# Seven of nine key chunks, and the pooled queries, turned from rounded copies, with other target times in the order: pooled attention and two MLPs on one core

## Chip, core and metric

One NeuronCore of a Trainium2 chip runs the whole program. The metric is the device time of one execution in microseconds (us). Three runs of the kernel before took 680.78, 680.83 and 681.04 us; the median is 680.83 us.

## What is computed

```python
batch, n_heads, seq, head_dim = (2, 8, 1152, 64)
# _attn_ref
q_pool = q.reshape(B, H, S // factor, factor, D).mean(axis=3)      # factor 2: 576 queries a head
scores = scale * np.matmul(q_pool, k.transpose(0, 1, 3, 2))
scores = scores - np.max(scores, axis=-1, keepdims=True)
attn = np.exp(scores)
attn = attn / (np.sum(attn, axis=-1, keepdims=True) + 1e-09)
out = np.matmul(attn, v)
# the heads are joined to x (1152 x 512), then two MLPs, 512 -> 2048 -> 512
h = x @ w_in;  g = 0 / ((h + 1)**2 / 4) / h by h <= -1, between, >= 1;  x = g @ w_out
h = x @ w_in;  g = h * sigmoid(h);  out = g @ w_out
```

## The kernel before

Every product is made in float32r from operands split into a rounded high part and a rest (`lo_of`, L138).

**Attention, 16 heads.** For a head, `inputs` (L409) loads q, k and v. K is rounded (L446) and its rest taken (L138), the nine chunks of 128 keys are turned by TensorE (L464) and evicted to `kk` (L469) by ScalarE or VectorE. Of the 576 pooled queries 512 are handled here: GpSimd adds the pairs (L481), a DMA doubles the sum beside itself in `qs` (L488), TensorE turns the four tiles of 128 queries in float32 (L496), and ScalarE and VectorE make `qm` of it (L499, L503). The remaining 64 queries of two heads form a tail tile (`pt`, `qts`, L526 to L537).

`scores` (L540) makes, per tile of 128 queries, three products of 384 keys (L570); VectorE evicts each to a tile `p` of 128 x 1152 and keeps the least value (L577, L587); ScalarE takes the exponent in place (L590). There are eight buffers `p`, four to a head. `values` (L618) then takes the nine key chunks c = 0 to 8: TensorE turns the four `p` tiles of a chunk into one bank, the bank is split into high part and rest (`split`, L600: ScalarE and VectorE, or ScalarE and GpSimd), and two products with V follow (L647).

A chunk is turned in one of two ways. Chunks 0 to 3 are turned straight from `p` in float32 (`turn`, L630). Chunks 4 to 8 are turned from a float32r copy (`turn_copy`, L634): after the exponent, SyncE sends two DMAs per tile (L597) that copy chunks 4, 5 to `pr0` and 6, 7, 8 to `pr1`. There is one buffer of each, so a head's copies wait until the head before has been turned from them:

```python
COPIED = ((4, 2), (6, 3))
prs = [pp.tile([P, NM, n * P], F32R, name=f"pr{i}") for i, (_, n) in enumerate(COPIED)]
copy = lambda i=i, c=c, n=n: nc.sync.dma_start(out=prs[i][:, t].bitcast(F32), in_=ps_[pb.slot][:, c * P : (c + n) * P])
```

**MLPs.** There are 96 steps of `gemm1` (L158) and `gemm2` (L203 in the first MLP, L205 in the second). The first four `gemm1` steps are laid between the last heads.

**What sets the order.** All of this is written as a list of operations (`op`, L276 on), each with a target time, the ways in which it can run (engine, occupancy, latency), what it depends on and the buffers it takes. `plan_out` (L262) is a list scheduler: on each engine it takes, among what can start at once, the operation with the least target, and each engine then runs its instructions in that fixed order. SyncE's row of DMA issues is one of these orders too: an issue that waits holds all behind it.

Of the kernel before, what the change touches and what calls it, by code (L numbers as in the profile page):

```python
# [1 line left out]

# [16 lines left out]
def fused_kernel(  # L19
# [11 lines left out]
    nc = tc.nc  # L31
# [22 lines left out]
    WARM = 7  # L54
    COPIED = ((4, 2), (6, 3))
    AHEAD = 3.0
# [208 lines left out]
    def plan_out():  # L265
# [78 lines left out]
    with ExitStack() as at, ExitStack() as keys, ExitStack() as prep:  # L344
# [15 lines left out]
        khls = several(nat, 2, [P, KC, 2, D], F32R, "khl")  # L360
        qss = several(nat, 2, [P, NM, 2, D], F32, "qs")
        kks = several(qk, 3, [P, KC, P], F32R, "kk")
        qms = [several(qk, 2, [P, NM * P], F32R, f"qm{i}") for i in range(2)]
        qts = [several(qk, 2, [P, 3, QT], F32R, f"qt{i}") for i in range(2)]
        ps_ = several(pp, 2 * NM, [P, S], F32, "p")
        pts = several(pp, 1, [P, S], F32, "pt")
# [8 lines left out]
        tiny = fixed.tile([P, 1], F32, name="tiny")  # L375
        room.update(qraw=2, kraw=2, vraw=1, khl=2, qs=2, kk=3, qm=2, qt=2, qtraw=2, qts=1, p=2 * NM, pt=1, **{f"pr{i}": 1 for i in range(len(COPIED))}, thl=THL, pf=PF, vhl=2)
        room.update(y2=2, rb=2, z=1, b=6, y=2, w=1)
# [28 lines left out]
        def base(h):  # L406
            return h * PERIOD

        def inputs(h):  # L409
# [5 lines left out]
            def load(which, dst, src):  # L415
                return lambda: nc.sync.dma_start(out=dst(), in_=src)

            kraw[h] = kr = Buf("kraw")
            queue = ("SP", 1.2, 3.9, nc.sync) if h else ("ACT", 0.1, 3.8, nc.scalar)
            lk = op(t0, (*queue[:3], lambda: queue[3].dma_start(out=kraws[kr.slot], in_=k[b, hd].rearrange("(p c) d -> p c d", c=KC))), bufs=[kr])  # L420
            qraw[h] = qr = Buf("qraw")
            lq = op(
                t0 - 0.1,
                ("SP", 1.1, 3.8, lambda: nc.sync.dma_start(out=qraws[qr.slot], in_=q[b, hd, 0 : 2 * NM * P].rearrange("(t p r) d -> p t r d", p=P, r=2))),
                bufs=[qr],
# [12 lines left out]
            tv = base(h - 2) + (6 if h < 3 else 0)  # L438
            lv = op(tv, ("SP", 1.2, 3.9, lambda: nc.sync.dma_start(out=vraws[vr.slot], in_=v[b, hd].rearrange("(p c) d -> p c d", c=KC))), bufs=[vr])

# [3 lines left out]
            for part in [slice(3 * g, 3 * g + 3) for g in range(3)] if h == 0 else [slice(0, KC)] * 1:  # L444
                n = (part.stop - part.start) / KC
                hi = lambda part=part: nc.scalar.copy(khls[kb.slot][:, part, 0], kraws[kr.slot][:, part])  # L446
                khi.append(op(t1, ("ACT", 0.08 + 0.5 * n, 0.17 + 0.51 * n, hi), [lk], [kr, kb]))
                lo = lambda e, part=part: lambda: lo_of(e, khls[kb.slot][:, part, 1], kraws[kr.slot][:, part], khls[kb.slot][:, part, 0])
                ways = [("POOL", 0.2 + 1.175 * n, 0.25 + 1.18 * n, lo(nc.gpsimd))]
                if not h:  # L450
                    ways.insert(0, ("DVE", 0.1 + 0.6 * n, 0.18 + 0.6 * n, lo(nc.vector)))
                klo.append(op(t1 + 0.01, ways, [khi[-1]], [kr, kb], both=not h))
# [21 lines left out]

            qb, bank, mb = Buf("qs"), Buf("b"), Buf("qm")
            qm[h] = mb

            def split_q(e):
                t = qraws[qr.slot]
                if h:  # L480
                    e.tensor_add(qss[qb.slot][:, :, 0], t[:, :, 0], t[:, :, 1])  # L481
                else:
                    e.tensor_add(qss[qb.slot], *(t[:, :, r].unsqueeze(2).to_broadcast([P, NM, 2, D]) for r in range(2)))

            t3 = base(h - 2) - 0.1 * PERIOD
            if h:
                sq = op(t3, ("POOL", 0.7, 0.76, lambda: split_q(nc.gpsimd)), [lq], [qr, qb])
                twice = lambda: nc.sync.dma_start(out=qss[qb.slot][:, :, 1], in_=qss[qb.slot][:, :, 0])  # L488
                sq = op(t3 + 1, ("SP", 0.5, 2.6, twice), [sq], [qb])
            else:  # L490
                sq = op(t3, [("DVE", 0.6, 0.69, lambda: split_q(nc.vector)), ("POOL", 1.25, 1.31, lambda: split_q(nc.gpsimd))], [lq], [qr, qb], both=True)
            t4 = base(h - 2) + 0.3 * PERIOD

            def turn_q():
                for i in range(NM):
                    nc.tensor.transpose(banks[bank.slot][:, i * P : (i + 1) * P], qss[qb.slot][:, i].rearrange("p a d -> p (a d)"), ident)  # L496

            o = op(t4, ("PE", 0.436, 0.6, turn_q), [sq], [qb, bank])
            o1 = op(t4 + 0.5, ("ACT", 0.483, 0.62, lambda: nc.scalar.mul(qms[mb.slot][0], banks[bank.slot], SCALE)), [o], [bank, mb])  # L499
# [40 lines left out]
        def scores(h, t):  # L540
# [53 lines left out]
            for i, (c, n) in enumerate(COPIED if not pair else ()):  # L594
                if not t:
                    pr_of[h, i] = Buf(f"pr{i}")
                copy = lambda i=i, c=c, n=n: nc.sync.dma_start(out=prs[i][:, t].bitcast(F32), in_=ps_[pb.slot][:, c * P : (c + n) * P])  # L597
                o_r[h, i, t] = op(base(h) + (c - 4) * STEP, ("SP", 0.2 + 0.18 * n, 2.7 + 0.2 * n, copy), [o_p[key, t]], [pb, pr_of[h, i]])

# [18 lines left out]
        def values(h):  # L618
# [5 lines left out]
            for c in range(KC):  # L624
# [12 lines left out]
                if x:  # L637
                    do = lambda x=x[0], f=turn_copy: f(x=x)
                    o = op(tc_, ("PE", 0.27, 0.45, do), [o_r[h, x[0], i] for i in range(NM)], [bank, pr_of[h, x[0]]])
                else:  # L640
                    o = op(tc_, ("PE", 0.436, 0.6, turn), [o_p[h, i] for i in range(NM)], [bank] + [p_of[h, i] for i in range(NM)])
# [67 lines left out]
        def invert(h):  # L709
# [26 lines left out]

            o = op(t0 + 0.5, ("SP", 0.4, 2.4, down), [o])
            o_inv[h] = op(t0 + 2.5, ("SP", 0.5, 4.2, up), [o], [rb])

# [64 lines left out]
        def weights(w, kind, times, deps):  # L804
# [14 lines left out]
            for n, t in enumerate(times):  # L819
                bufs = [Buf("w" if (w, kind) == (0, "i") else "raw" if w else "eraw"), *whole]  # L820
                bank = Buf("b")
                if not w:
                    via[n] = lambda bank=bank: banks[bank.slot]
                prev = op(t - 5, ("SP", 2.0, 4.4, lambda n=n: get(n, 0)()), [*deps, w_last[0]], bufs)
                w_last[0] = prev
                for m, (e, occ, lat) in enumerate(STAGES if w else FAR):
                    more = bufs if w or not m else [*bufs, bank]
                    prev = op(t + 0.3 * m, (e, occ, lat, lambda n=n, m=m: get(n, m + 1)()), [prev], more, both=e == "DVE" and w > 0)
                prev = op(t + 2, ("ACT", 0.51, 0.61, lambda n=n: get(n, 7)()), [prev], bufs)
                made.append(op(t + 2.1, ("POOL", 1.25, 1.3, lambda n=n: get(n, 8)()), [prev], bufs))  # L830
# [124 lines left out]
```

## Time and profile before

| | |
|---|---|
| profiled execution | 680.63 us |
| its span | 678.5 us (2.13 us lie around it) |
| median of three runs | 680.83 us |
| TensorE (PE) busy | 670.0 us, 99% |
| VectorE, ScalarE, GpSimd busy | 524.0, 420.2, 438.0 us |
| TensorE's mean granted clock | 0.997 |

A row of a timeline gives start, length, engine, line, operation, out<-in and how many were merged. Matmuls overlap in the records: the recorded length of one is longer than the time after which the next one starts, so what a group of products costs TensorE is read from one start to the next. In brackets stands idle time before a row and what ended it. PEld is the weight load of TensorE, which runs beside the products.

### The profile page before, as it was taken

The numbers are of one execution on the slowest core, as the hardware profiler recorded it, in microseconds if no ns is written. First come the engines' busy times: TensorE is split into PE (matmuls) and PEld (weight loads), VectorE is DVE, ScalarE is ACT, GpSimd is POOL, SyncE is SP. The second block draws the span as 40 slices with busy tenths as digits, with TensorE's granted clock in tenths as the row PEclk, the third lists the DMA queues.
The fourth block names the chain that finished last, engine by engine and source line by source line (L and its number), as shares of the span: only waits on it lengthen the run. The fifth ranks groups of instructions, "written<-read, shape, count | busy, mean of one in ns | idle before, by whom it ended". The sixth has DMA issues, their size and how long they took to land.

```text
span 678.5 us, 11815 instructions
## 1 busy us (share of the span) xinstructions
PE 670.0 (99%) x3962; PEld 623.5 (92%) x3962; DVE 524.0 (77%) x1180; ACT 420.2 (62%) x808; POOL 438.0 (65%) x414
## 2 busy tenths in 40 slices
PE   8999999999999999999999999999999999999997
PEld 6899988999999979999999999999999999999996
DVE  6879898988888898389898995996983794892223
ACT  5989998999898888455644443455554543442221
POOL 5788999999797878546646453486853553553221
PEclk8999999999999999999999999999999999999999
DMA  7866655645433356113333231231231331300012
GB/s 214 213 212 177 188 165 169 179 145 173 130 115 109 98 167 205 47 63 109 110 103 117 93 122 34 95 95 61 94 125 37 116 98 38 118 1 0 1 48 93
DMA packets 54988, 75.90 MB, mean 112 GB/s; under 512 B 14736, under 2 KB 40592, under 8 KB 54928
## 3 DMA queue, kind: packets, MB, share of 16 engines
q1 hardware_dynamic: 54640, 74.73, 35.3%
q8 instruction: 31, 0.51, 0.3%
q10 hardware_dynamic: 288, 0.43, 0.2%
q14 instruction: 29, 0.24, 0.1%
HBM read 49.81 MB, written 2.39 MB: 77 GB/s over the span
## 4 chain that ended last, share of the span: by engine, by line
PE 94%; DVE 2%; DMA 2%; ACT 1%; issue 1%; DVEq 0%; ACTq 0%
PE bank L158 30%; PE bank L203 15%; PE bank L205 15%; PE bank L570 12%; PE bank L647 10%; PE bank L630 4%; PE bank L634 3%; PE bank L685 3%; PE bank L464 1%; PE bank L676 1%; DMA pr<-p 1%; PE bank L496 1%; DMA qraw<-in_q_dram 1%; DVE p L577 0%; DVE part L217 0%
## 5 line engine op out<-in xcount | busy, mean ns | idle before, releaser
L138 POOL TENSOR_TENSOR gl<-gf,gh 128x384 fp32r<-128x384 f32 x96 | 110.0, 1147 | 107.3 <-ACT gh L187 104.0
L158 PE MATMUL bank<-xh,whi 128*128 128x384 f32 x384 | 129.7, 338 | 0.0
L158 PE MATMUL bank<-xh,wli 128*128 128x384 f32 x384 | 129.2, 337 | 0.0
L158 PE MATMUL bank<-xl,whi 128*128 128x384 f32 x384 | 129.2, 336 | 0.0
L577 DVE TENSOR_SCALAR_CACHE_REDUCE p<-bank 128x384 f32<-128x384 f32 x192 | 102.0, 551 | 20.7 <-PE bank L570 14.3
L647 PE MATMUL bank<-thl,vhl 128*128 128x512 f32 x288 | 113.4, 429 | 0.0
L138 POOL TENSOR_TENSOR thl<-pf,thl 128x512 fp32r<-128x512 f32 x80 | 103.7, 1298 | 4.0 <-PE bank L647 0.7
L181 DVE TENSOR_TENSOR gf<-bank,gf 128x384 f32<-128x384 f32 x96 | 52.9, 551 | 65.0 <-ACT gf L173 60.6
L570 PE MATMUL bank<-kk,qm 128*128 128x384 f32 x384 | 97.3, 357 | 0.3
L590 ACT ACTIVATE p<-p,low 128x1152 f32<-128x1152 f32 x64 | 81.5, 1274 | 2.7 <-DVE low L587 2.6
L187 ACT CAST gh<-gf 128x384 fp32r<-128x384 f32 x96 | 49.3, 513 | 49.6 <-DVE gf L181 47.6
L158 PEld LDWEIGHTS bank<-xl,whi 128*128 128x128 f32 x384 | 72.1, 188 | 4.2
L158 PEld LDWEIGHTS bank<-xh,whi 128*128 128x128 f32 x384 | 72.1, 188 | 4.0
L138 POOL TENSOR_TENSOR wli<-wf,whi 128x512 fp32r<-128x512 f32 x32 | 43.8, 1369 | 45.6 <-ACT whi L128 45.5
L570 PEld LDWEIGHTS bank<-kk,qm 128*128 128x128 f32 x384 | 66.4, 193 | 7.2 <-DVE thl L609 1.2
L158 PEld LDWEIGHTS bank<-xh,wli 128*128 128x128 f32 x384 | 72.1, 188 | 0.0
L138 POOL TENSOR_TENSOR wlo<-wf,who 128x512 fp32r<-128x512 f32 x32 | 44.0, 1374 | 37.3 <-ACT who L128 37.3
L173 ACT ACTIVATE gf<-bank 128x384 f32<-128x384 f32 x48 | 23.6, 491 | 70.8 <-PE bank L158 64.9
L116 DVE SCALAR_TENSOR_TENSOR wf<-wr,wf 128x512 uint32<-128x512 uint32 x56 | 65.0, 1160 | 1.0
L203 PE MATMUL bank<-gh,wlo 128*128 128x384 f32 x192 | 65.0, 338 | 0.0
L203 PE MATMUL bank<-gh,who 128*128 128x384 f32 x192 | 64.8, 337 | 0.0
L203 PE MATMUL bank<-gl,who 128*128 128x384 f32 x192 | 64.7, 337 | 0.0
(97 smaller groups left out, 1550.8 us busy)
## 6 DMA issues: line engine op xcount, KB each, us to landing
wr<-in_moe_w_in_dram SPq DMA_DIRECT2D x32, 512.0 KB, 3.7
wr<-in_moe_w_out_dram SPq DMA_DIRECT2D x32, 512.0 KB, 3.3
pr<-p SPq DMA_DIRECT2D x64, 192.0 KB, 2.3
pr<-p SPq DMA_DIRECT2D x64, 128.0 KB, 2.2
vraw<-in_v_dram SPq DMA_DIRECT2D x16, 288.0 KB, 3.3
kraw<-in_k_dram SPq DMA_DIRECT2D x15, 288.0 KB, 3.3
qraw<-in_q_dram SPq DMA_DIRECT2D x16, 256.0 KB, 3.4
rb<-row SPq DMA_DIRECT2D x16, 128.0 KB, 3.1
```

Source lines behind the costliest of these rows:

```text
L116: nc.vector.scalar_tensor_tensor(xi, st["top"], 0xC0000000, xi, ALU.bitwise_and, ALU.bitwise_or)
L138: eng.tensor_sub(out, whole, hi.bitcast(F32))
L158: nc.tensor.matmul(ps, lhsT=w[:, c, j * P : (j + 1) * P], rhs=a[:, c, ts_], start=(c == 0 and n == 0), stop=(c == ND - 1 and n == 2),)
L181: nc.vector.tensor_tensor(gf, hps.pop(i), gf, op=ALU.mult if steps[i][0] else ALU.max)
L187: nc.scalar.copy(gh, gf)
L203: nc.tensor.matmul(ps[:, :TB], lhsT=w[:, j, m * P : (m + 1) * P], rhs=a, start=start, stop=stop)
L205: nc.tensor.matmul(ps[:, cols], lhsT=a[:, m * P : (m + 1) * P], rhs=w[:, j, cols], start=start, stop=stop)
L570: nc.tensor.matmul(ps, lhsT=qq[:, c0 : c0 + P], rhs=rhs, start=n == 0, stop=n == last)
L577: nc.vector.tensor_scalar(dst, ps, -1.0, None, ALU.mult, ALU.min, accum_out=mxs[key, t][:, j : j + 1])
L590: nc.scalar.activation(pt(), pt(), AF.Exp, bias=lows[key][:, tt : tt + 1], scale=-1.0, accum_out=sums[key][:, tt : tt + 1])
L630: nc.tensor.transpose(banks[bank.slot][:, i * P : (i + 1) * P], ps_[p_of[h, i].slot][:, c * P : (c + 1) * P], ident)
L647: nc.tensor.matmul(banks[6 + yb.slot], lhsT=lhsT, rhs=thls[tb.slot][i], start=not count, stop=len(count) == 2 * KC - 1)
```

## The change

- `COPIED` becomes ((2, 3), (5, 4)): chunks 2 to 8 are turned from float32r copies, chunks 0 and 1 straight from `p`. There are still two DMAs per tile, now of three and four chunks.
- The buffers `p` are six instead of eight.
- The pair sums go to a tile `qs` of 256 columns; for heads 1 to 15 two DMAs copy it to both halves of a float32r tile `qd`, from which TensorE turns with the float32r identity. Head 0 uses a buffer of `y2` and is turned in float32 as before.
- The rounding of K may run on VectorE as well (heads 1 to 15).
- Each operation's target gets a random amount between -1 and +1 us (seed 51).
- The scheduler's figures for DMA issues and for turns from copies are others.

```diff
-    COPIED = ((4, 2), (6, 3))
+    STAGED, COPIED = 6, ((2, 3), (5, 4))
+    KWAYS = 2
+    SEED, SPREAD = 51, 1.0
...
+        if SPREAD:
+            rnd = Random(SEED)
+            for o in ops:
+                o.target += rnd.uniform(-SPREAD, SPREAD)
...
-        qss = several(nat, 2, [P, NM, 2, D], F32, "qs")
+        qss = several(nat, 2, [P, NM, D], F32, "qs")
+        qds = several(nat, 2, [P, NM, 2, D], F32R, "qd")
...
-        ps_ = several(pp, 2 * NM, [P, S], F32, "p")
+        ps_ = several(pp, STAGED, [P, S], F32, "p")
...
-                khi.append(op(t1, ("ACT", 0.08 + 0.5 * n, 0.17 + 0.51 * n, hi), [lk], [kr, kb]))
+                ways = [("ACT", 0.08 + 0.5 * n, 0.17 + 0.51 * n, hi), ("DVE", 0.08 + 0.28 * n, 0.17 + 0.28 * n, lambda part=part: nc.vector.tensor_copy(khls[kb.slot][:, part, 0], kraws[kr.slot][:, part]))]
+                khi.append(op(t1, ways[: KWAYS if h else 1], [lk], [kr, kb], both=True))
...
-                    e.tensor_add(qss[qb.slot][:, :, 0], t[:, :, 0], t[:, :, 1])
+                    e.tensor_add(qss[qb.slot], t[:, :, 0], t[:, :, 1])
...
-                twice = lambda: nc.sync.dma_start(out=qss[qb.slot][:, :, 1], in_=qss[qb.slot][:, :, 0])
-                sq = op(t3 + 1, ("SP", 0.5, 2.6, twice), [sq], [qb])
+                twice = lambda: [nc.sync.dma_start(out=qds[qb2.slot][:, :, x].bitcast(F32), in_=qss[qb.slot]) for x in range(2)]
+                sq = op(t3 + 1, ("SP", 1.3, 3.9, twice), [sq], [qb, qb2])
...
-                    nc.tensor.transpose(banks[bank.slot][:, i * P : (i + 1) * P], qss[qb.slot][:, i].rearrange("p a d -> p (a d)"), ident)
+                    to = banks[bank.slot][:, i * P : (i + 1) * P]
+                    if h:
+                        nc.tensor.transpose(to.bitcast(F32R), qds[qb2.slot][:, i].rearrange("p a d -> p (a d)"), ident_r)
+                    else:
+                        nc.tensor.transpose(to, first_q[:, i].rearrange("p a d -> p (a d)"), ident)
...
-                o_r[h, i, t] = op(base(h) + (c - 4) * STEP, ("SP", 0.2 + 0.18 * n, 2.7 + 0.2 * n, copy), [o_p[key, t]], [pb, pr_of[h, i]])
+                o_r[h, i, t] = op(base(h) + (c - 4) * STEP, ("SP", 0.6, 2.5 + 0.15 * n, copy), [o_p[key, t]], [pb, pr_of[h, i]])
...
-                    o = op(tc_, ("PE", 0.27, 0.45, do), [o_r[h, x[0], i] for i in range(NM)], [bank, pr_of[h, x[0]]])
+                    o = op(tc_, ("PE", 0.35, 0.53, do), [o_r[h, x[0], i] for i in range(NM)], [bank, pr_of[h, x[0]]])
```

How the order moves is shown at three places. Lines of the changed kernel are larger by 11 to 15 here: L645 turns from `p` (before L630), L649 from a copy (L634), L592 evicts scores (L577), L612 copies `p` to `pr` (L597), L479 evicts K (L469).

VectorE in the first 20 us, while the first head's scores are evicted (`p_121` to `p_124` are its four tiles before, `p_123` to `p_126` after; `kk_111` and `kk_113` are the second head's keys). Before:

```order
L577 TENSOR_SCALAR p_122,mx<-bank_72 128x384
L587 TENSOR_REDUCE low<-mx 128x1
L577 TENSOR_SCALAR p_122,mx<-bank_73 128x384
L469 CAST kk_111<-bank_75 128x384
L577 TENSOR_SCALAR p_122,mx<-bank_70 128x384
L469 CAST kk_111<-bank_71 128x384
```

Now:

```order
L592 TENSOR_SCALAR p_124,mx<-bank_72 128x384
L602 TENSOR_REDUCE low<-mx 128x1
L592 TENSOR_SCALAR p_124,mx<-bank_70 128x384
L592 TENSOR_SCALAR p_124,mx<-bank_74 128x384
L592 TENSOR_SCALAR p_125,mx<-bank_75 128x384
L602 TENSOR_REDUCE low<-mx 128x1
```

Two evictions of keys stood between those of the second tile; now one stands later, after the first eviction of the fourth tile, and the other is on ScalarE.

SyncE's issues for the eleventh head (four copies to each of `pr_130` and `pr_131`, the two copy buffers). Before:

```order
L597 DMA pr_130<-p_121 128x256
L597 DMA pr_130<-p_122 128x256
L597 DMA pr_130<-p_123 128x256
L597 DMA pr_131<-p_121 128x384
L597 DMA pr_131<-p_122 128x384
```

Now:

```order
L612 DMA pr_130<-p_125 128x384
L612 DMA pr_130<-p_127 128x384
L612 DMA pr_130<-p_123 128x384
L612 DMA pr_131<-p_123 128x512
L612 DMA pr_131<-p_127 128x512
L612 DMA pr_131<-p_125 128x512
```

The copies are as many, each a chunk longer, and stand at the same place of the row; the buffers `p_121` to `p_128` have become `p_123` to `p_128`.

TensorE at the straight turns of that head, now, up to the next head's third tile (`kk_112,qm_117` are the twelfth head's keys and queries, `thl` the split chunks). Before, four groups like the two of L645 stood here.

```order
L645 MATMUL bank_75<-ident,p_123 128x128
L645 MATMUL bank_75<-ident,p_128 128x128
L662 MATMUL bank_77<-thl_136,vhl_142 128x512
L645 MATMUL bank_72<-ident,p_125 128x128
L645 MATMUL bank_72<-ident,p_127 128x128
L645 MATMUL bank_72<-ident,p_123 128x128
L645 MATMUL bank_72<-ident,p_128 128x128
L662 MATMUL bank_77<-thl_133,vhl_142 128x512
L585 MATMUL bank_70<-kk_112,qm_117 128x384
L585 MATMUL bank_70<-kk_112,qm_118 128x384
L585 MATMUL bank_73<-kk_112,qm_117 128x384
L585 MATMUL bank_73<-kk_112,qm_118 128x384
```

The last product here fills `bank_73`, which VectorE evicts into `p_123`, the buffer that the last straight turn has just read and that the copy to `pr_131` must have read too.

## Rows read from the trace of the kernel before

**Rows 1.** The page: busy time of TensorE, and the main DMA queue.

```profile
PE 670.0 (99%) x3962; PEld 623.5 (92%) x3962; DVE 524.0 (77%) x1180; ACT 420.2 (62%) x808; POOL 438.0 (65%) x414
...
q1 hardware_dynamic: 54640, 74.73, 35.3%
```

**Rows 2.** Stretches: length, busy time of each engine, granted clock, DMA share, GB/s.

```profile
0.00:20.00 20.00, 16.94 (x83) 13.73 (x84) 14.54 (x50) 13.17 (x25) 12.83 (x23) 0.91 0.75 215
240.00:260.00 20.00, 18.52 (x117) 16.10 (x116) 18.48 (x60) 17.23 (x32) 15.95 (x16) 1.00 0.54 164
320.00:678.50 358.50, 354.80 (x1882) 335.05 (x1880) 257.53 (x383) 153.69 (x293) 177.92 (x147) 1.00 0.23 76
...
20.00:260.00 240.00, 238.24 (x1641) 216.05 (x1642) 207.91 (x678) 218.80 (x424) 210.86 (x213) 1.00 0.53 160
```

**Rows 3.** Waits of TensorE, the longest in the attention: total, times, longest.

```profile
PE bank L634 <- DVE wf L120: 0.6, 1, 0.6
```

**Rows 4.** Groups of instructions: the two kinds of turn.

```profile
L630 PE MATMUL bank<-ident,p 128*128 128x128 f32 x256 | 37.2, 273 | 0.3 <-DVE p L577 0.3
L634 PE MATMUL bank<-ident_r,pr 128*128 128x128 f32 x320 | 37.0, 239 | 0.7 <-DVE wf L120 0.6
```

**Rows 5.** Timeline of TensorE, 124 to 130 us.

```profile
124.14 0.51 PE L634 MATMUL bank<-ident_r,pr 128*128 128x128 f32 x4
124.48 0.47 PE L647 MATMUL bank<-thl,vhl 128*128 128x512 f32 x1
...
127.93 0.46 PE L634 MATMUL bank<-ident_r,pr 128*128 128x128 f32 x4
128.22 0.47 PE L647 MATMUL bank<-thl,vhl 128*128 128x512 f32 x1
128.53 0.51 PE L570 MATMUL bank<-kk,qm 128*128 128x384 f32 x2
128.88 0.60 PE L630 MATMUL bank<-ident,p 128*128 128x128 f32 x4
129.24 0.95 PE L570 MATMUL bank<-kk,qm 128*128 128x384 f32 x4
```

**Rows 6.** Tile `pr`: its DMAs (issue, ns; landing), and their landing at 20 to 40 us.

```profile
L597 SPq DMA_DIRECT2D pr<-p x128: 464/521/1817, 14.1 to 262.3; - x128
DMA to landing us min/median/max: 1.9/2.3/5.6
...
pr<-p SPq DMA_DIRECT2D x5, 192.0 KB, 3.7
```

**Rows 7.** Tile `qs`: its DMAs, their landing, and GpSimd's wait.

```profile
L488 SPq DMA_DIRECT2D qs<-qs x15: 619/628/697, 7.5 to 199.6; - x15
...
  PE bank L496: 6.4, 6
...
DMA to landing us min/median/max: 2.3/3.1/4.4
```

**Rows 8.** Groups: rounding of K, and evictions of K on ScalarE and VectorE.

```profile
L446 ACT CAST khl<-kraw 128x576 fp32r<-128x576 f32 x15 | 10.3, 689 | 1.9 <-POOL khl L138 1.0 <-PE bank L464 0.6 <-DMA vraw<-in_v_dram 0.3
L469 ACT CAST kk<-bank 128x384 fp32r<-128x384 f32 x19 | 9.0, 480 | 2.3 <-PE bank L464 2.2
...
L469 DVE CAST kk<-bank 128x384 fp32r<-128x384 f32 x29 | 16.0, 551 | 1.1 <-PE bank L464 0.9 <-ACT sum L716 0.2
```

**Rows 9.** Timeline of the first 26 us.

```profile
12.56 0.56 DVE L469 CAST kk<-bank 128x384 fp32r<-128x384 f32 x1 [0.69 <-PE bank L464]
...
20.90 2.14 PE L630 MATMUL bank<-ident,p 128*128 128x128 f32 x16
```

**Rows 10.** Timeline at the hand-over from attention to the MLP.

```profile
281.25 0.39 PE L647 MATMUL bank<-thl,vhl 128*128 128x512 f32 x1
...
284.89 1.29 POOL L138 TENSOR_TENSOR xl<-y,xh 128x512 fp32r<-128x512 f32 x1 [3.84 <-ACT xh L754]
...
287.20 0.34 PE L158 MATMUL bank<-xh,whi 128*128 128x384 f32 x1
```

More of the change, by code (lines that the diff above doesn't have):

```diff
@@ L1 @@
 from contextlib import ExitStack
+from random import Random
 import concourse.bass as bass
@@ L375, in fused_kernel @@
         tiny = fixed.tile([P, 1], F32, name="tiny")
-        room.update(qraw=2, kraw=2, vraw=1, khl=2, qs=2, kk=3, qm=2, qt=2, qtraw=2, qts=1, p=2 * NM, pt=1, **{f"pr{i}": 1 for i in range(len(COPIED))}, thl=THL, pf=PF, vhl=2)
+        room.update(qraw=2, kraw=2, vraw=1, khl=2, qs=2, qd=2, kk=3, qm=2, qt=2, qtraw=2, qts=1, p=STAGED, pt=1, **{f"pr{i}": 1 for i in range(len(COPIED))}, thl=THL, pf=PF, vhl=2)
         room.update(y2=2, rb=2, z=1, b=6, y=2, w=1)
@@ L418, in inputs @@
             kraw[h] = kr = Buf("kraw")
-            queue = ("SP", 1.2, 3.9, nc.sync) if h else ("ACT", 0.1, 3.8, nc.scalar)
+            queue = ("SP", 0.65, 3.9, nc.sync) if h else ("ACT", 0.1, 3.8, nc.scalar)
             lk = op(t0, (*queue[:3], lambda: queue[3].dma_start(out=kraws[kr.slot], in_=k[b, hd].rearrange("(p c) d -> p c d", c=KC))), bufs=[kr])
@@ L423, in inputs @@
                 t0 - 0.1,
-                ("SP", 1.1, 3.8, lambda: nc.sync.dma_start(out=qraws[qr.slot], in_=q[b, hd, 0 : 2 * NM * P].rearrange("(t p r) d -> p t r d", p=P, r=2))),
+                ("SP", 0.65, 3.8, lambda: nc.sync.dma_start(out=qraws[qr.slot], in_=q[b, hd, 0 : 2 * NM * P].rearrange("(t p r) d -> p t r d", p=P, r=2))),
                 bufs=[qr],
@@ L438, in inputs @@
             tv = base(h - 2) + (6 if h < 3 else 0)
-            lv = op(tv, ("SP", 1.2, 3.9, lambda: nc.sync.dma_start(out=vraws[vr.slot], in_=v[b, hd].rearrange("(p c) d -> p c d", c=KC))), bufs=[vr])
+            lv = op(tv, ("SP", 0.65, 3.9, lambda: nc.sync.dma_start(out=vraws[vr.slot], in_=v[b, hd].rearrange("(p c) d -> p c d", c=KC))), bufs=[vr])
             kb = khl[h] = Buf("khl")
@@ L473, in inputs @@
                 o_k[h].append(op(t2 + 0.5, ways, [o], [bank, kb2]))
-            qb, bank, mb = Buf("qs"), Buf("b"), Buf("qm")
+            qb, qb2, bank, mb = Buf("qs"), Buf("qd"), Buf("b"), Buf("qm")
+            first_q = y2s[0].rearrange("p (t a d) -> p t a d", a=2, d=D)
             qm[h] = mb
@@ L480, in split_q @@
                 if h:
-                    e.tensor_add(qss[qb.slot][:, :, 0], t[:, :, 0], t[:, :, 1])
+                    e.tensor_add(qss[qb.slot], t[:, :, 0], t[:, :, 1])
                 else:
-                    e.tensor_add(qss[qb.slot], *(t[:, :, r].unsqueeze(2).to_broadcast([P, NM, 2, D]) for r in range(2)))
+                    e.tensor_add(first_q, *(t[:, :, r].unsqueeze(2).to_broadcast([P, NM, 2, D]) for r in range(2)))
             t3 = base(h - 2) - 0.1 * PERIOD
@@ L495, in turn_q @@
                 for i in range(NM):
-                    nc.tensor.transpose(banks[bank.slot][:, i * P : (i + 1) * P], qss[qb.slot][:, i].rearrange("p a d -> p (a d)"), ident)
-            o = op(t4, ("PE", 0.436, 0.6, turn_q), [sq], [qb, bank])
+                    to = banks[bank.slot][:, i * P : (i + 1) * P]
[3 more added lines that the diff above has]
+                        nc.tensor.transpose(to, first_q[:, i].rearrange("p a d -> p (a d)"), ident)
+            o = op(t4, ("PE", 0.35, 0.53, turn_q) if h else ("PE", 0.436, 0.6, turn_q), [sq], [qb2 if h else qb, bank])
             o1 = op(t4 + 0.5, ("ACT", 0.483, 0.62, lambda: nc.scalar.mul(qms[mb.slot][0], banks[bank.slot], SCALE)), [o], [bank, mb])
@@ L735, in up @@
                 )
-            o = op(t0 + 0.5, ("SP", 0.4, 2.4, down), [o])
-            o_inv[h] = op(t0 + 2.5, ("SP", 0.5, 4.2, up), [o], [rb])
+            o = op(t0 + 0.5, ("SP", 0.6, 2.6, down), [o])
+            o_inv[h] = op(t0 + 2.5, ("SP", 0.6, 4.0, up), [o], [rb])
         def finish(h):
@@ L823, in weights @@
                     via[n] = lambda bank=bank: banks[bank.slot]
-                prev = op(t - 5, ("SP", 2.0, 4.4, lambda n=n: get(n, 0)()), [*deps, w_last[0]], bufs)
+                prev = op(t - 5, ("SP", 0.7 if w == 0 else 2.0, 5.0, lambda n=n: get(n, 0)()), [*deps, w_last[0]], bufs)
                 w_last[0] = prev
```

## The prediction

> **What bounds the kernel now.** I read the busy times first, then the same by stretches, then TensorE's waits, then its timeline. TensorE is busy for 99% of the span [rows 1], and by stretches it is full nearly everywhere: 238.24 of 240 us between 20 and 260 us, where ScalarE, GpSimd and VectorE stand at 218.80, 210.86 and 207.91 [rows 2]. Its longest wait in the attention is 0.6 us, once [rows 3]. So the bound is TensorE's own work, and what the change takes off it shows in the time, as long as the three engines behind it, each 9 to 13% below it, keep up. Two stretches are not full: the first 20 us, where it works 16.94 us, and 240 to 260 us, where it works 18.52 and so idles 1.5 us [rows 2]. From 320 us on the MLPs run without a break that a change in the attention could close; their instructions are the same in number, and I take that stretch as fixed.
>
> What a group costs is read from starts, since the recorded lengths overlap. In one unbroken piece of the timeline [rows 5] a turn of four blocks from a float32r copy starts at 127.93 and the next product at 128.22: 0.29 us. A turn of four from float32 starts at 128.88 and its successor at 129.24: 0.36. A product with V costs 0.31 behind a turn and a pair of score products 0.35 [rows 5].
>
> **The change, part by part.**
>
> *Turns.* Chunks 2 and 3 go over to copies: 2 x 16 = 32 groups of four, where today 64 are float32 and 80 float32r (256 and 320 products) [rows 4]. The queries of heads 1 to 15 add 15 groups. 47 groups x (0.36 - 0.29) = 3.3 us less work on the bounding engine. At worst a turn from a copy costs what the one at 124.14 did, 0.34 [rows 5], and 47 x 0.02 leaves 0.9 us; no row has one below 0.29. I take 3.3, as most such groups in that part of the timeline take 0.29.
>
> A rule speaks for far more. The Trainium skill, "FP8 and Floating Point Precision", section TensorE Precision Notes, says that true float32 takes four passes through the array. By it a float32r group would cost a quarter of 0.36, and 47 groups would give 12.7 us; the trace has both kinds side by side at 0.36 and 0.29, and the measurement decides [rows 5].
>
> *Copies of p.* They are 128 DMAs as before, of three and four chunks instead of two and three: 4 x 448 KB a head for 4 x 320 KB. An issue takes SyncE 0.52 us, and the data land after 2.3 us, 5.6 at the longest, 3.7 in the crowded stretch from 20 to 40 us [rows 6]. The added bytes are 16 x 0.5 MB and, for the second copy of the queries, 15 x 0.125 MB, some 10 MB. The main queue moved 74.73 MB in 35.3% of the span [rows 1], so they add about 4.8% of it, 32 us of DMA time, and the share of 0.53 between 20 and 260 us [rows 2] becomes an estimated 0.66. Nobody queues behind that for long; I cost it at nothing on the path. The cover is TensorE's other work between exponent and turn: in the shown order, where a chunk from a copy is ready only after issue and landing, four or more groups stand between.
>
> *Six buffers instead of eight.* This is the edit with a new wait in it. The copy to `pr1` can be issued only when the head before has been turned from `pr1`, and the buffer can be overwritten only when that copy has landed. I counted TensorE's rows between that last turn and the score product whose eviction overwrites the buffer, and priced them by [rows 5]. Before, never less than 15 us lie there. Now the third tile of most heads has between 4.6 and 8.4 us. The least is the twelfth head's, at the third place shown of the order: seven pairs of scores (2.45), two straight groups (0.72), four products with V (1.0), two tail products and a turn of keys (0.4, an estimate from their columns), 4.6 us. The chain needs 0.52 + 2.3 = 2.8 us there [rows 6], so 1.8 us are left, and 2.3 to 3.0 us for the next four. I cost the edit at nothing; below zero it can't go, above it is a rival. If the cover is gone, VectorE stands at the eviction with all the splits queued behind it, and TensorE waits for banks.
>
> *Queries.* The two DMAs take SyncE 2 x 0.63 us instead of once, and land 0.63 us later than today's 3.1 [rows 7]. TensorE never waited for one after the start; it turns a head's queries microseconds later. A gain lies beside it: GpSimd waited 6.4 us for TensorE to free `qs` [rows 7], and the new `qs` is free when the copies have landed. GpSimd isn't the bound, so nothing. Against it, a turn that waits for two transfers may pay for one more wait at the sequencer: up to 0.05 x 15 = 0.75 us, taken as nothing.
>
> *ScalarE and VectorE.* By the order, VectorE takes three of the 15 roundings of K from ScalarE, and ScalarE takes eight evictions of K. ScalarE: 8 x 0.480 - 3 x 0.689 = 1.8 us more; VectorE: 8 x 0.551 = 4.4 us less, and three roundings that no row shows there, between nothing and the 0.689 of ScalarE, 2.1 us for all [rows 8]. Both hide behind TensorE on average (218.80 + 1.8 of 240).
>
> *The start.* The first turn, at 20.90 us, waits for the fourth tile's exponent, and that for VectorE's chain of evictions. The first place shown of the order takes two evictions of keys out of it, of which one comes back before the fourth tile is done: 0.55 us less, and the 0.69 us that VectorE stood waiting for TensorE's turn of those keys goes with them [rows 9]. Between 0 and 1.2 us; I take 0.6, half, since K of the second head is now needed earlier on ScalarE.
>
> *Hand-over.* The first MLP product that needs all heads starts at 287.20, 5.95 us after the last product with V at 281.25; the last piece it needs is ready at 284.89 + 1.29 = 286.18 [rows 10]. In the new order TensorE has more work between these two, by one group of the second product, so the gain is not lost there.
>
> *Moved targets.* They put every engine's order anew. No row prices that: it can close the 1.5 us idle at 240 to 260 us, or open such stretches [rows 2]. I take 0.
>
> **Sum:** -3.3 - 0.6 = -3.9 against the profiled execution's 680.63 (span 678.5 and 2.13 around it): 676.7. The median stands 0.2 us higher, so **676.9 us**.
>
> **Rivals.** A measurement of this kernel can tell about 0.2%, 1.4 us, from no change.
>
> 1. *The new order also closes idle time of the old one.* The 1.5 us of 240 to 260 us, and half of what the first 20 us still lack ((20 - 16.94) / 2 = 1.5) [rows 2]: 676.9 - 3.0 = 673.9. For it: these gaps belong to one order. Against: nothing in the order shows that they go. 0.12.
>
> 2. *Four passes.* If the new turns cost a quarter of the float32 ones, 680.8 - 12.7 - 0.6 = 667.5. The starts at 127.93 and 128.22 speak against it [rows 5]: 0.01.
>
> 3. *The order opens as much as the turns save.* Two stretches like 240 to 260 us cost 3.0 us [rows 2]: 679.9, no change. For it: the waits there came from VectorE's weight work between attention's, and the targets of all of it are moved. Against: between 20 and 240 us an order of the same scheduler leaves next to no idle time. 0.13.
>
> 4. *ScalarE becomes the bound* (slower). It stands at 91% of 20 to 260 us, gets 1.8 us more, and TensorE gets faster around it. If ScalarE's chain sets the length of a head, the turns save nothing and the 1.8 us come on top: 682.6. It decides once ScalarE has no idle time left in the attention; it has 21 us of 240 now [rows 2], so this needs them to lie where they can't be used. 0.10.
>
> 5. *VectorE waits for landings* (slower). The slack left in the tightest tiles is 1.8, 2.3, 2.8, 2.9, 3.0, 3.4, 3.5, 3.8 and 3.9 us. If every copy landed after 5.6 us, the worst of the rows [rows 6], 3.3 us more than now, these would lack 1.5 + 1.0 + 0.5 + 0.4 + 0.3 = 3.7 us, which eats the gain. At 6.0 us they lack 6.2 us in all: 683.1. So it decides from a landing of about 5.6 us; the median is 2.3, and 3.7 at its most crowded. 0.08.
>
> **How the numbers follow.** Forecast 0.56, rivals 0.12, 0.01, 0.13, 0.10, 0.08. Faster by over 0.2%: 0.56 + 0.12 + 0.01 = 0.69; within 0.2%: 0.13; slower: 0.18. Of 2 in 10 left out I put half above and half below: the top takes in rival 4 with the extra wait of the queries up to 682.8, the bottom rival 1, to 673.4. The forecast's own range is 675.5 (all of the start's 1.2 us and half of the 1.5 us idle) to 679.3 (the turns at 0.34).
>
> **What would show it.** Right: 32 and 15 groups more of float32r turns at 0.29 us from start to start, TensorE as full as now between 20 and 260 us, the first straight turn before 20.9 us, the MLPs from 320 us unchanged in length, and no wait of VectorE's evictions for `pr`. Rival 5 would show as such waits, and as idle TensorE before scores; rival 4 as ScalarE above 95% in the attention with TensorE's groups waiting for split chunks; rival 3 as new idle stretches of TensorE behind VectorE. The prediction is wrong if the turns save their 3.3 us and the span doesn't fall.

## The result, and the profile after

The changed kernel takes 688.89 us in the median of four runs, against 680.81 us for the kernel before: 1.012 times as long, with a 95% interval from 1.0107 to 1.0133. The forecast was 676.9 us; it is 8.1 us slower instead of 3.9 us faster. The execution shown here took 688.93 us, its span is 687.1 us.

The page's busy row, and the main DMA queue, as in [rows 1]:

```profile
PE 670.7 (98%) x3962; PEld 622.0 (91%) x3962; DVE 512.9 (75%) x1175; ACT 422.3 (61%) x813; POOL 438.3 (64%) x414
...
q1 hardware_dynamic: 62560, 85.09, 40.4%
```

The stretches (length, busy time of each engine, granted clock, DMA share, GB/s), to be read against [rows 2]:

```profile
20.00:40.00 20.00, 17.88 (x113) 15.75 (x113) 14.68 (x53) 15.81 (x32) 13.59 (x14) 0.91 0.98 277
60.00:80.00 20.00, 18.30 (x125) 16.01 (x123) 17.37 (x54) 17.66 (x35) 17.66 (x19) 1.00 0.78 215
120.00:140.00 20.00, 17.52 (x116) 15.21 (x116) 15.79 (x52) 16.47 (x34) 16.05 (x16) 1.00 0.69 206
20.00:260.00 240.00, 231.18 (x1594) 207.40 (x1593) 199.30 (x646) 211.86 (x414) 202.15 (x205) 0.99 0.66 193
328.60:687.10 358.50, 354.80 (x1885) 335.22 (x1883) 252.04 (x385) 155.93 (x294) 181.05 (x148) 1.00 0.24 78
```

The last 358.5 us, the MLPs, hold 354.80 us of TensorE's work, exactly as before. In the attention TensorE was full for 238.24 of 240 us and is now for 231.18: 7 us of new idle time, in a few places. Its waits between 20 and 290 us say what for (total, times, longest):

```profile
PE bank L662 <- POOL thl L141: 4.3, 4, 1.6
PE bank L662 <- POOL thl L629: 2.4, 1, 2.4
PE bank L662 <- DMA pr<-p: 0.6, 1, 0.6
```

The products with V wait 6.7 us for the split parts `thl` that GpSimd makes. GpSimd itself is busy for only 64% of the span. Its own waits from the start to 290 us:

```profile
POOL thl L629 <- ACT pf L628: 12.5, 10, 2.1
POOL qs L492 <- DMA qd<-qs: 8.3, 4, 3.8
POOL qs L492 <- PE bank L585: 3.9, 2, 2.3
...
POOL qs L492 <- PE bank L474: 2.2, 1, 2.2
POOL qs L492 <- DMA qraw<-in_q_dram: 1.6, 2, 1.1
```

At the pair sum (L492) it stands for 16.0 us in all. Before, it stood there 6.4 us for TensorE's turns [rows 7]; now what it mostly stands for is the landing of the copies `qd<-qs`. One of the waits, the 2.2 us put down to L474 (at 33.48 us), is still there with more buffers and is then put down to the load of q (e1), so about 12 us belong to the two buffers. The worst place, on its timeline with SyncE's issue of those copies and the product that waits (start, length, engine, line, operation):

```profile
122.95 1.31 SPq L499 DMA_DIRECT2D qd<-qs  x2
...
125.00 1.30 POOL L141 TENSOR_TENSOR thl<-pf,thl 128x512 fp32r<-128x512 f32 x1
...
130.09 0.72 POOL L492 TENSOR_TENSOR qs<-qraw 128x256 f32<-128x256 f32 x1 [3.79 <-DMA qd<-qs]
130.77 1.51 POOL L764 TENSOR_TENSOR y<-y,rb 128x512 f32<-128x512 f32 x1
...
132.23 0.61 POOL L629 CAST thl<-pf 128x512 fp32r<-128x512 f32 x1
...
132.89 0.50 PE L662 MATMUL bank<-thl,vhl 128*128 128x512 f32 x1 [2.45 <-POOL thl L629]
```

The split at 132.23 needs nothing of the queries. It stands behind the pair sum on GpSimd, and the sum stands for a buffer that is free only when copies of a sum made two heads earlier have landed. Those copies in turn were issued only when TensorE's turn of an earlier head's queries (L509) had freed a `qd`. The chain of waits over the same stretch says it in one view:

```profile
122.63 0.29 PE bank L509 x4
...
123.18 0.41 SPq L499
123.58 0.05 issue
123.64 6.32 DMA qd<-qs
...
130.09 0.04 POOL qs L492
...
130.77 1.51 POOL y L764
132.28 0.56 POOL thl L629
...
132.89 0.50 PE bank L662
```

From the first issue at 122.95 to the landing at 129.96 the pair takes 7.0 us; the scheduler's figure for both is 3.9 (the line of `twice` in the diff). At 62.72 us the sum waits 2.34 us; the profile puts that down to TensorE's scores, but the chain there has `DMA qd<-qs` for 3.73 us, then 2.33 us that it puts down to nothing, then the sum. With more buffers for the sums this wait goes too (e1). Landing by name (size, median), where [rows 7] had 3.1 and [rows 6] 2.3:

```profile
pr<-p SPq DMA_DIRECT2D x64, 256.0 KB, 3.1
...
pr<-p SPq DMA_DIRECT2D x64, 192.0 KB, 3.0
...
qd<-qs SPq DMA_DIRECT2D x30, 128.0 KB, 4.3
```

### The profile page after: what moved, and what is told of

Read it like the earlier page. It is cut to its first block, busy times and chain, and to the rows that moved or that the text cites. A ratio compares the mean times of both kernels' runs of the same rounds, so it can differ in the third digit from the quotient of the medians.

```text
span 687.1 us, 11820 instructions
## 1 busy us (share of the span) xinstructions
PE 670.7 (98%) x3962; PEld 622.0 (91%) x3962; DVE 512.9 (75%) x1175; ACT 422.3 (61%) x813; POOL 438.3 (64%) x414
## 3 DMA queue, kind: packets, MB, share of 16 engines
q1 hardware_dynamic: 62560, 85.09, 40.4%
## 4 chain that ended last, share of the span: by engine, by line
PE 87%; DMA 5%; DVE 3%; POOL 1%; issue 1%; ACT 1%; SPq 1%; DVEq 0%; POOLq 0%; ACTq 0%
PE bank L161 29%; PE bank L206 15%; PE bank L208 14%; PE bank L585 9%; PE bank L662 8%; PE bank L649 4%; DMA qd<-qs 4%; PE bank L700 2%; PE bank L645 2%; DVE p L592 1%; DMA pr<-p 1%; PE bank L474 1%; PE bank L691 1%; POOL thl L141 1%; DMA qraw<-in_q_dram 1%
## 5 line engine op out<-in xcount | busy, mean ns | idle before, releaser
L662 PE MATMUL bank<-thl,vhl 128*128 128x512 f32 x288 | 111.5, 427 | 7.7 <-POOL thl L141 4.3
L592 DVE TENSOR_SCALAR_CACHE_REDUCE p<-bank 128x384 f32<-128x384 f32 x192 | 101.1, 552 | 18.5 <-PE bank L585 15.9
L585 PE MATMUL bank<-kk,qm 128*128 128x384 f32 x384 | 96.2, 357 | 0.9 <-ACT pf L628 0.5
L585 PEld LDWEIGHTS bank<-kk,qm 128*128 128x128 f32 x384 | 67.0, 193 | 6.9 <-ACT pf L628 1.1
L662 PEld LDWEIGHTS bank<-thl,vhl 128*128 128x128 f32 x288 | 51.5, 189 | 11.3 <-POOL thl L141 6.1
L624 DVE TENSOR_TENSOR thl<-bank,thl 128x512 fp32r<-128x512 f32 (+1 forms) x88 | 56.3, 648 | 6.8 <-ACT thl L623 6.4
```

Of the source, the lines that this page charges most:

```text
L585: nc.tensor.matmul(ps, lhsT=qq[:, c0 : c0 + P], rhs=rhs, start=n == 0, stop=n == last)
L592: nc.vector.tensor_scalar(dst, ps, -1.0, None, ALU.mult, ALU.min, accum_out=mxs[key, t][:, j : j + 1])
L624: o2 = op(target + 0.3, ("DVE", 0.6 * f, 0.683 * f, lambda: nc.vector.tensor_sub(tl(), ps(), th().bitcast(F32))), [o1], [bank, tb])
L662: nc.tensor.matmul(banks[6 + yb.slot], lhsT=lhsT, rhs=thls[tb.slot][i], start=not count, stop=len(count) == 2 * KC - 1)
```

## The experiments

Each run is compared with runs of the kernel before on the same chip, so the ratios are compared; times are medians, and a difference in us is a ratio's distance from 1 times 680.3. The theories are: 1, the pair sum's wait for landed copies; 2, the added bytes of the copies of `p` and the six buffers; 3, the moved targets; 4 (from e8 on), the scheduler's smaller figures for loads.

**e1: the same order, four buffers for the sums.** After the plan is made, the buffers of `qs` are dealt out anew over four tiles; no instruction moves.

```diff
-        qss = several(nat, 2, [P, NM, D], F32, "qs")
+        qss = several(nat, 4, [P, NM, D], F32, "qs")
...
         order = plan_out()
+        for i, b in enumerate(dict.fromkeys(b for o in order for b in o.bufs if b.group == "qs")):
+            b.slot = i % 4
```

> The changed kernel with the same order of every instruction and four buffers for the pair sums instead of two, so that GpSimd's pair sum need not wait until the copies of the sum two heads before have landed. Theory 1 (GpSimd stands at the pair sum with the splits queued behind it): the waits of the pair sum for the copies (8.3 us, and some 6 us put down to TensorE) go, TensorE's waits at the products with V for GpSimd's splits (6.7 us) mostly with them, 681 to 684 us. Theory 2 (the added bytes of the copies of p and the six buffers): the waits move elsewhere, 687 to 690. Theory 3 (the moved targets put splits and scores in an unlucky order): 686 to 690, the products with V still wait.

679.15 us, 0.999 (0.9981 to 1.0). Against the changed kernel's 1.012 that is 8.8 us, from one buffer count. At the place shown above GpSimd now runs on; its split follows SyncE's issue of the copies by 5.5 us instead of 9.3. Timeline of e1:

```profile
120.83 1.31 SPq L499 DMA_DIRECT2D qd<-qs  x2
...
124.11 0.74 POOL L492 TENSOR_TENSOR qs<-qraw 128x256 f32<-128x256 f32 x1
124.81 1.57 POOL L764 TENSOR_TENSOR y<-y,rb 128x512 f32<-128x512 f32 x1
...
126.32 0.62 POOL L629 CAST thl<-pf 128x512 fp32r<-128x512 f32 x1
```

The copies still land after 4.1 us in the median and 6.5 at most, and no sum waits for them. What GpSimd still stands for at the sum is the load of q, and TensorE's waits for GpSimd's splits are down to one:

```profile
POOL qs L492 <- DMA qraw<-in_q_dram: 4.2, 3, 2.4
...
PE bank L662 <- POOL thl L141: 1.5, 1, 1.5
```

and its stretches where the changed kernel stopped are full:

```profile
60.00:80.00 20.00, 20.00 (x142) 18.18 (x141) 19.29 (x61) 19.70 (x39) 19.83 (x21) 1.00 0.81 237
120.00:140.00 20.00, 20.00 (x144) 18.23 (x142) 18.70 (x60) 19.40 (x40) 19.51 (x21) 1.00 0.76 214
```

Theory 1 is shown; its forecast of 681 to 684 was too careful by 2 us.

**e2: the queries as before** (sum and copy in one tile, one DMA, a float32 turn; the rest as changed, planned anew).

> The changed kernel with the queries handled as before (the sum and its copy in one tile, one transfer, a float32 turn); copies of seven chunks, six buffers, moved targets stay. The order is planned anew. Theory 1: GpSimd no longer stands for landed copies, TensorE has 15 x 0.07 = 1.1 us more work than in the changed kernel, 678 to 683. Theory 2: 686 or more. Theory 3: 686 or more, since the targets are moved as much as in the changed kernel.

681.71 us, 1.0007 (0.9996 to 1.0018): 7.7 us faster than the changed kernel, with 1.1 us more work on TensorE. This agrees with theory 1 and speaks against 2 and 3.

**e3: no moved targets** (`SPREAD = 0.0`).

> The changed kernel without the moved targets, all else as changed; the order is planned anew. Theory 1: the pair sums still wait for landings, 685 to 690. Theory 2: 685 to 690. Theory 3: the time comes back to what the turns alone would give, 676 to 681.

683.62 us, 1.0056 (1.0039 to 1.0074). Neither forecast holds. In this order GpSimd stands at the pair sum for only 0.9 us, so the two buffers need an order that calls for the sum just as its copies land; and the kernel is slow all the same. From 20 to 40 us its TensorE works 18.15 of 20 us (20.00 before); what causes that was not separated.

**e4: the kernel before with the copies of seven chunks and six buffers alone** (and the scheduler's figures for these copies and turns).

```diff
-    COPIED = ((4, 2), (6, 3))
+    STAGED, COPIED = 6, ((2, 3), (5, 4))
...
```

> The kernel before with seven copied chunks, six buffers of p and the new figures for these copies and turns alone; queries, targets and the rounding of K as before. TensorE has 32 x 0.07 = 2.2 us less work than before. Theory 1: 677 to 681. Theory 2: the landings get as long as in the changed kernel (3.0 us) and TensorE stops for them, 684 to 690. Theory 3: 677 to 681.

679.09 us, 0.998 (0.9971 to 0.9988): faster than before by 1.4 us, though its copies land after 2.7 us in the median. No kernel here that computes the reference's output has a lower ratio, but the intervals of e1, e5, e16 and e17 overlap with this one. Theory 2 falls as the cause of the loss.

**e5: the kernel before with moved targets alone.**

> The kernel before with nothing changed but the targets, moved by the same seed. Theory 1 (the pair sum's wait for landed copies is the loss, the moved targets only shift it): within 2.5 us of before, 679 to 683, with no long wait of GpSimd at the pair sum. Theory 3 (this set of moved targets is bad in itself): 684 to 690.

679.49 us, 0.9987 (0.9975 to 0.9999). In the kernel before, this set of moved targets costs nothing; as the loss by itself, theory 3 falls.

**e6 and e7: another seed, with two and with four buffers for the sums**, the same order in both (`SEED = 52`; e7 with the diff of e1).

> The changed kernel with another seed for the moved targets (52 instead of 51) and still two buffers for the pair sums. Theory 1: the wait belongs to the two buffers and the landing after 4 us, so it comes with another order too: several us of GpSimd's waits for landed copies, 682 to 690. If the waits came only by the chance of seed 51, GpSimd waits less than 2 us for copies and the time is 677 to 682.

> The order of the run with seed 52, instruction by instruction, with four buffers for the pair sums. Theory 1: faster than that run by about what TensorE waited there for GpSimd's splits, 2 to 8 us, to 677 to 682. If seed 51 alone was unlucky: within 1 us of the run with seed 52.

683.31 us, 1.004 (1.0027 to 1.0054), and 680.47 us, 1.0 (0.9992 to 1.0009): 2.7 us from the buffers alone. GpSimd's waits at the sum, of e6:

```profile
POOL qs L492 <- DMA qraw<-in_q_dram: 4.2, 2, 2.4
...
POOL qs L492 <- DMA qd<-qs: 1.3, 1, 1.3
POOL qs L492 <- PE bank L649: 1.1, 1, 1.1
```

and of e7:

```profile
POOL qs L492 <- DMA qraw<-in_q_dram: 2.7, 3, 1.0
```

The direction is as forecast. The waits in e6 are smaller than "several us for copies": 1.3 us, below the 2 us named for mere chance, though the time lies in the range of theory 1. So seed 51 was unlucky in size, not in kind.

**e8 and e9: queries as before, no moved targets; then with the old figures for the loads too.**

```diff
-            queue = ("SP", 0.65, 3.9, nc.sync) if h else ("ACT", 0.1, 3.8, nc.scalar)
+            queue = ("SP", 1.2, 3.9, nc.sync) if h else ("ACT", 0.1, 3.8, nc.scalar)
```

> The changed kernel with the queries as before and without moved targets: beside the copies of seven chunks and the six buffers only the two ways for the rounding of K and the scheduler's other figures for loads are left. Against the run with copies alone it tells what these two are worth. Theory 1: they cost nothing, 678 to 681, as with the copies alone. Theory 4 (the smaller figures for the loads crowd the first 40 us with transfers, and TensorE stops there): 681 to 685, with TensorE below 19 of 20 us between 20 and 40 us.

> The run with queries as before and without moved targets (683.46), with the scheduler's old figures for the loads of q, k and v (SyncE held 1.1 to 1.2 us for each, instead of 0.65); the rounding of K may still run on VectorE. Beside the copies alone (679.09) only that rounding differs. Theory 4 (the figures for the loads crowd the first 40 us): 678 to 681. If the two ways for the rounding of K are what costs 4.4 us: 682 to 685.

683.46 us, 1.0035 (1.002 to 1.0049), and 680.84 us, 1.0006 (0.9997 to 1.0014). The old figures give 2.0 us back, but not in the way theory 4 has it: in e8 TensorE works 19.21 of the 20 us from 20 to 40 us, not under 19, and the DMA share of the first 40 us is 0.84 and 0.81 in the two. That the transfers of the start are the cause is not shown.

**e10, e11, e12: four buffers planned for** (`room` says four for `qs`), old load figures, K rounded on ScalarE alone; not moved, moved by seed 51, and with fewer copies for the first two heads.

> All that the change does to chunks and queries, planned for four buffers of the pair sums, with the old figures for the loads, K rounded on ScalarE alone and no moved targets. TensorE has 3.3 us less work than before and 1.05 us less than with the copies of seven chunks alone (679.09). Theory 1 with theory 4: no wait for the copies of the sums, and the first 40 us as with the copies alone, 676 to 679.5. Theory 2 (the second copy of the sums and the landings of 4 us cost elsewhere): 680 to 685.

> The same with the targets moved by seed 51. Theory 1 with theory 4: within 2 us of the one that is not moved, 676 to 681. Theory 3 (these targets are bad in themselves): 683 or more.

> As the one with four buffers, old load figures and no moved targets, but the first two heads copy chunks 5 to 8 only and turn chunks 0 to 4 straight: 1.5 MB less to move in the first 40 us, against six float32 groups more on TensorE (0.4 us). If the crowded transfers stop TensorE there: 0.5 to 3 us faster than the one with all copies. If they don't: 0 to 1 us slower.

682.45 us, 1.0033 (1.0023 to 1.0044); 681.88 us, 1.0026 (1.0015 to 1.0036); 685.38 us, 1.0072 (1.0054 to 1.009). e11 (by 0.9 us) and e12 miss. e10 misses the range of theories 1 and 4 and lies in the other, but not for the reason named there: the copies of the sums land after 2.9 us in the median, and nobody waits for them. e10 has nothing left of the sum's wait and is still 3.6 us slower than e4, which differs in the queries and in some of the scheduler's figures (for weights and for the sums' rows; the expectation of e9 overlooked these too). In e12 fewer transfers made it slower: its longest wait, 2.2 us for `pr`, lies at 267 us, far from the two heads whose copies were cut. What a new order brings is as large here as what was being tested.

**e13: e1 with the 47 new groups turned in float32**, from the same copies, in the same order.

```diff
-                        nc.tensor.transpose(to.bitcast(F32R), qds[qb2.slot][:, i].rearrange("p a d -> p (a d)"), ident_r)
+                        nc.tensor.transpose(to, qds[qb2.slot][:, i].bitcast(F32).rearrange("p a d -> p (a d)"), ident)
```

(and likewise for chunks 2 and 3)

> The run with the changed order and four buffers for the sums (679.15), instruction by instruction, with the 47 groups that the change turned in float32r (chunks 2 and 3, the queries of heads 1 to 15) turned in float32 from the same copies. If a float32r group saves 0.07 us on the bounding engine, as the prediction has it: 3.3 us slower, 682 to 683. If the turns save less than was read from the starts, or TensorE has to wait anyway: under 1.5 us slower.

682.15 us, 1.0026 (1.0016 to 1.0035): 2.4 us slower than e1, between 1.1 and 3.7 by the ends of the two intervals. The turns are worth about what they were taken for, with 3.3 us inside these ends.

**e14 and e15: e1 with smaller copies of `p`**, for two heads and for all but the first.

```diff
-                copy = lambda i=i, c=c, n=n: nc.sync.dma_start(
+                copy = lambda i=i, c=c, n=(1 if h in (1, 2) else n): nc.sync.dma_start(
...
```

> The run with the changed order and four buffers for the sums, with the copies of the second and third head cut to one chunk each; the other chunks of those heads are turned from what the head before left in the buffer, so the output of these heads is not the reference's. Same instructions, same waits, 2.5 MB less to move, most of it between 20 and 50 us. If the crowded transfers there stop TensorE (it lost 8.9 us between 20 and 60 us against 4.0 before): 2 to 5 us faster. If not: within 1 us.

> The same with the copies of all heads but the first cut to one chunk each, 19 MB less to move: chunks 3, 4 and 6 to 8 of those heads are turned from what the first head left, so their output is not the reference's. If the transfers take back what the turns save: 675 to 677. If only the crowded start does: as the run before, within 1 us. If neither: 678 to 680.

679.11 us, 0.9983 (0.9974 to 0.9992), and 678.64 us, 0.9971 (0.996 to 0.9982). The 8.9 and 4.0 us named there are the time from start to start of TensorE's instructions between 20 and 60 us, beyond what the same groups take where nothing interrupts them. Taking 2.5 MB away in the crowded stretch gains 0.5 us on e1, within what can't be told apart. Taking two thirds of the copied bytes away (the main queue moves 65.43 MB instead of 85.09) gains 1.3 us, with intervals that just touch (0.9981 and 0.9982). In e15 the copies land after 2.1 us. So by the medians some 20 MB cost 1.3 us (between nothing and 2.7 by the ends of the intervals), and the 10 MB that the change added cost less than that; that they take back what the turns save is not shown.

**e16, e17, e18: three more orders of e4** (its targets moved by seeds 51, 52, 53).

> The kernel before with copies of seven chunks, six buffers and the figures for them, as in the run with copies alone (679.09), with the targets moved by seed 51; queries and loads as before. Theory 1 with theory 4: no waits for copied sums and no crowded start, within 2 us of the run with copies alone, 677 to 681. Theory 3: 682 or more.

> The kernel before with copies of seven chunks, six buffers and the figures for them, targets moved by seed 52. TensorE has 2.2 us less work than before; what another order adds or saves is not known: 676.5 to 681.5. If this one and the next lie within 1 us of 679.09 and 680.01, the order hardly matters where nothing waits for copied sums; if they scatter by 2 us or more, it matters as much as the turns.

> The same with seed 53: 676.5 to 681.5, read together with the run before.

680.01, 679.35 and 681.64 us; 0.9992 (0.9984 to 1.0001), 0.9989 (0.998 to 0.9998) and 1.0022 (1.0013 to 1.0031). With e4's 0.998 the four orders of the same work span 0.42%, 2.9 us; e18 lies 0.1 us above its range. None beats e4.

## Why the prediction was wrong, point by point

**The step that failed is "Queries".** It said of GpSimd's wait for `qs`: "the new qs is free when the copies have landed. GpSimd isn't the bound, so nothing". The first half names the right event, and the sums do run further ahead: the one at 130.09 us waits for copies that followed the turn four heads before its own, where before a sum waited for the turn two heads before. But it counts the landing as a gain. By its own figures, 3.1 and 0.63 us more, the pair would have landed 3.7 us after the first issue; at the place shown it took 7.0, and the sum stood for it. The second half cost the time: an engine that is busy only 64% of the time still holds up whoever needs what it has yet to do. The splits of the next chunk are queued behind the sum, and TensorE waits for them. For VectorE the prediction did price a wait by the splits queued behind it (rival 5); for GpSimd it took the average load. e1 measures the step at 8.8 us, between 7.3 and 10.3 by the ends of the intervals.

**Turns.** The 47 groups run as read: 0.28 us from start to start for queries and 0.29 for a copied chunk, as in

```profile
208.18 0.45 PE L509 MATMUL bank<-ident_r,qd 128*128 128x128 f32 x4
208.46 0.47 PE L662 MATMUL bank<-thl,vhl 128*128 128x512 f32 x1
208.77 0.45 PE L649 MATMUL bank<-ident_r,pr 128*128 128x128 f32 x4
209.06 0.42 PE L474 MATMUL bank<-ident_r,khl 128*128 128x128 f32 x3
```

and e13 gives them 2.4 us for the 3.3 forecast. Right within the interval; the four passes of rival 2 (12.7 us) are out. The prediction read one pair of groups; the medians over such groups without a stop in the trace before are 0.35 us (48 groups) and 0.29 (76), which gives 2.8 us. The extra wait at the sequencer, 0.05 us, stands before 6 of the 15 turns of queries; the 15 take 0.30 us from start to start in the median, so it hardly shows.

**Copies of `p`.** The estimate of the DMA share was right (0.66 between 20 and 260 us), the landing was not: 3.0 to 3.1 us instead of 2.3. "At nothing" was nearly right: by e15, where about twice the added bytes are gone, the median is 1.3 us faster than e1.

**Six buffers.** Right: no eviction of VectorE's waits for a copy to `pr`, and TensorE's longest waits at its scores (L585) are 0.5 us. Rival 5 did not come.

**ScalarE, VectorE.** Right in effect: 27 evictions of K on ScalarE (19 before), three roundings on VectorE at 743 ns, above the 0.689 that was to bound them. ScalarE stands at 211.86 of 240 us, so rival 4 did not come either.

**Start and hand-over.** The first straight turn starts at 20.57 us instead of 20.90: 0.3 us of the 0.6. From the last product with V (289.39) to the first MLP product that needs all heads (295.87) it is 6.5 us, against 5.95 before [rows 10]; the stretch after it is unchanged.

**Moved targets.** "I take 0" holds for the kernel before (e5), but not as a term apart: they decide whether the sum meets its copies (e3, e6 and the changed kernel wait 0.9, 2.7 and some 12 us there for something other than the load of q). The idle time at 240 to 260 us did close as in rival 1: TensorE works 19.92 of these 20 us, and 19.43 from 248 to 268 us, where about the same work now lies. New idle stretches came as in rival 3, but behind GpSimd instead of VectorE, and more than twice as long as the 3 us priced there.

**The sum.** The forecast missed by 12.0 us. The pair sum's wait is 8.8 of it. Of the other 3.2, the turns' shortfall is 0.9 and the start's 0.3, neither much above its uncertainty, and the other 2.0 us lie within the 2.9 us by which orders of the same work differ. The trace of e1, whose execution took 681.3 us, 2.1 above its median, says where to look. TensorE works 236.19 of 240 us there between 20 and 260 us, against 238.24 before, and more than the whole difference lies between 20 and 40 us. The stretch before, and in e1:

```profile
20.00:40.00 20.00, 20.00 (x136) 17.68 (x137) 16.30 (x54) 19.24 (x39) 16.44 (x18) 1.00 0.86 229
```

```profile
20.00:40.00 20.00, 16.89 (x111) 14.62 (x109) 14.59 (x50) 15.89 (x31) 13.64 (x15) 0.93 1.01 275
```

One stop in it is the same queue once more, now for the load of q by the profile, where more buffers of the sums do not help:

```profile
33.26 0.73 POOL L492 TENSOR_TENSOR qs<-qraw 128x256 f32<-128x256 f32 x1 [2.40 <-DMA qraw<-in_q_dram]
...
35.27 0.49 PE L662 MATMUL bank<-thl,vhl 128*128 128x512 f32 x1 [1.52 <-POOL thl L141]
```

Full DMA engines alone are not shown to cause it: in e15 the DMA share of these 20 us is 0.85, as before, and TensorE works 17.44 of them. What holds up the start in this order is open. That a larger figure for the pair of copies in the scheduler would have kept the sum out of the way is likely, but was not tried.

Two figures of the prediction do not follow from its rows: four products with V are put at 1.0 us, where its 0.31 for each gives 1.24, and the outer ends of the range, 682.8 and 673.4, are not the sums of the terms named. Neither changes the outcome.

## What to carry to other kernels

Price a wait on an in-order engine by what is queued behind it and who needs that, however idle the engine is on average. When a step is split into a producer, a transfer and a consumer, the first buffer's lifetime becomes issue plus landing: give it more buffers (two more did it here), or, which was not tried, tell the scheduler the landing that the trace shows, for the whole group of transfers. To separate an edit from the new order that a scheduler makes of it, keep the order and change only the buffers: here the scatter of orders (2.9 us) is as large as the gain that was sought (3.3 us).

## What was not expected of the hardware

Of the copies within SBUF the query copies are the smallest, and the slowest to land. Before, 128 KB of them took 3.1 us [rows 7] where 128 KB of `pr` took 2.2 us; in the changed kernel they take 4.3 us and 256 KB of `pr` 3.1 us. The row of before:

```profile
pr<-p SPq DMA_DIRECT2D x64, 128.0 KB, 2.2
```

Both go from SBUF to SBUF on the same queue; the sums' copies go in pieces of 256 bytes, the copies to `pr` in pieces of 1 KB and more. The Trainium skill, "DMA: Bandwidth & Descriptors", section "Why small descriptors are slow (HBM only)", says that transfers from SBUF to SBUF do not suffer from small pieces. The trace of the kernel before does not agree: a piece of 256 bytes occupies its DMA engine for 18 ns in the median (7680 pieces), one of 1 KB for 46 ns (8192), so the small ones take 1.6 times as long for the same bytes. Spread evenly over 16 engines that would be 0.58 us against 0.37 for 128 KB, an estimate from these two medians, and only 0.2 of the 0.9 us by which the landings differ. What makes up the rest no run here shows.

In e1 TensorE idled at 33.8 to 35.3 us and for 0.7 us more up to 40 us. Its granted clock fell between 35 and 40 us and stayed low while the engine was full (columns as above, PE first, the granted clock third from the end):

```profile
30.00:35.00 5.00, 3.75 (x25) 3.16 (x23) 3.43 (x12) 2.37 (x7) 2.60 (x4) 1.00 1.07 317
35.00:40.00 5.00, 4.03 (x22) 3.15 (x22) 2.17 (x7) 4.47 (x9) 4.07 (x6) 0.73 1.08 307
40.00:45.00 5.00, 5.00 (x23) 4.40 (x23) 2.72 (x8) 3.78 (x7) 4.07 (x5) 0.58 0.73 177
45.00:50.00 5.00, 5.00 (x41) 4.71 (x40) 4.68 (x12) 3.79 (x9) 3.61 (x5) 1.00 0.45 145
```

From 40 to 45 us it is busy throughout at 0.58, so mostly at the lower level, 1.2 GHz, and a turn of four blocks takes 0.47 us from start to start (42.54 to 43.01) where it takes 0.29 at 46.30. The changed kernel has the same drop there (0.66 from 35 to 40 us, also after a stop). Its longer stop at 130.4 to 132.9 us has no such consequence: its stretch from 120 to 140 us is at 1.00. After a stop the clock can be low for longer than the stop lasted, and is not so each time; what decides it no run here shows.
